# Layer 2's tokens are stored unsummed, and each pass forms Strassen's sums on the chip

## The chip, the core and the metric

The kernel runs on one NeuronCore of one Trainium2 chip. The time is the device time of one execution in microseconds (us). Engines are named as in the profile: PE is TensorE (matmuls; PEld its weight loads), DVE is VectorE, ACT is ScalarE, POOL is GpSimd, SP is the engine whose queue issues every DMA.

## What is computed

Attention in chunks of 64 feeds two gated MLPs, all in float32:

```python
scores = scale * np.matmul(q_c, k_c.transpose(0, 1, 2, 4, 3))   # 8 heads, chunks of 64
attn = softmax(scores)
x = np.matmul(attn, v_c)              # reshaped to 4608 tokens x 512
g = x @ w_gate                        # layer 1: 512 -> 1536 -> 512
x = (g * sigmoid(g)) * (x @ w_val) @ w_out
h = x @ w_in                          # layer 2: 512 -> 2048 -> 512
out = (h * sigmoid(1.702 * h)) @ w_out2
```

## The kernel before

The 4608 tokens are worked on in 9 blocks of 512 (numbers 0 to 8). There are four passes over the blocks: passes 0 and 1 are the two halves of layer 1's hidden width, passes 2 and 3 those of layer 2's. In the trace pass 0 runs to about 460 us (with the attention inside it), pass 1 to about 960 us, pass 2 to about 1290 us, pass 3 to the end. A pass has three groups of weights per block in layer 1 and two in layer 2.

Matrix products are done by Strassen's scheme (Winograd's form): a product of 2x2 quarters takes seven products of quarters or of sums of quarters, labelled "1" to "7". Each float32 operand is split into a high and a low part (`hi` is a rounded copy in float32r, `lo` is the rest), and `mm3` (L628 to L630) makes three matmuls of each pair of operands: hi x hi, hi x lo, lo x hi. So a block's tokens appear as seven tiles `xs` (ring `x`, seven places, one set), each with a hi and a lo half.

What happens to layer 2's tokens before the change: at the end of each block of pass 1 the block lies in `xr`, and `x_to_dram` makes the seven operands. `token_combos` does four subtractions (DVE, L620 and L1048), then each of the seven gets a copy (hi, on ACT, L616, into the staging area `sp`) and a subtraction (lo, in place), and both halves are stored to `x_dram[1]`: 14 stores of 256 KB. Block 7 is an exception: its seven tiles stay in `xs` as pass 2 starts with it. In passes 2 and 3 `x_load` fetches seven tiles of 512 KB for each other block. The area `sp` is also where layer 1's hidden values get their hi and lo halves for the second product (`hidden_part`).

Second weights: a layer 2 pass has two groups, each with seven tiles of second weights of 512 KB (`od_b`). Those of the first group are held for the pass in `WO` (places `wa2`, `wb2`, `wc6` to `wc8`); those of the second group are fetched for every block through the three buffers of ring `o`. In pass 1 the second weights come the same way (`o<-yw_dram`).

While pass 1 runs, layer 2's weights are also converted from the host's form and stored (`group_to_dram`: raw loads, ACT and DVE work, hi and lo into ring `ws` of two buffers, stores `wd_b` and `od_b`); the weights of pass 3 are converted during pass 2.

The order of the instructions is set by a planner (`Program`): every operation is recorded with an engine, a cost, a due time and its dependences, the planner orders each engine's queue, and the table `PLACES` then moves single operations by number ("behind:what" for each engine, and so also from one engine to another). Each engine runs its queue strictly in that order.

Of the kernel before, what the change touches and what calls it, by code (L numbers as in the profile page):

```python
# [9 lines left out]
F32 = mybir.dt.float32  # L10
F32R = mybir.dt.float32r
# [8 lines left out]
P = 128  # L20
# [3 lines left out]
def rd(ap):  # L24
# [1731 lines left out]
```

## Time and profile before

| what | value |
|---|---|
| time, median of 3 runs | 1671.15 us (1670.75 to 1671.49) |
| profiled execution | 1678.61 us, its span 1676.8 us, mean granted clock 0.997 |
| busy share of PE, DVE, ACT, POOL | 98%, 77%, 54%, 31% |
| moved by DMA | 511.85 MB, mean 305 GB/s |

The profiled execution is 7.46 us longer than the median of the runs; differences of the two kernels are taken on the profiled one and carried over. "Busy" of PE is from a model of pipelined matmuls; a stretch in which PE runs without a hole shows its busy time equal to its length, and the number of instructions in it then gives PE's full pace.

### The profile page before, as it was taken

The numbers are of one execution on the slowest core, as the hardware profiler recorded it, in microseconds if no ns is written. First come the engines' busy times: TensorE is split into PE (matmuls) and PEld (weight loads), VectorE is DVE, ScalarE is ACT, GpSimd is POOL, SyncE is SP. The second block draws the span as 40 slices with busy tenths as digits, with TensorE's granted clock in tenths as the row PEclk, the third lists the DMA queues.
The fourth block names the chain that finished last, engine by engine and source line by source line (L and its number), as shares of the span: only waits on it lengthen the run. The fifth ranks groups of instructions, "written<-read, shape, count | busy, mean of one in ns | idle before, by whom it ended". The sixth has DMA issues, their size and how long they took to land. (4 is left out here: it accounts for less than half of the span.)

```text
span 1676.8 us, 38536 instructions
## 1 busy us (share of the span) xinstructions
PE 1639.5 (98%) x15254; PEld 1604.5 (96%) x15254; DVE 1292.6 (77%) x2061; ACT 902.6 (54%) x1574; POOL 517.7 (31%) x505
## 2 busy tenths in 40 slices
PE   8999999999999999999999999999999999999998
PEld 7898999999999999999999999999999999999998
DVE  7998888888887788888887878787865565555556
ACT  6976776767644444445443455566534444444443
POOL 2432433142012311342220232545642133333333
PEclk9999999999999999999999999999999999999999
DMA  7589989998999999999999998898869877777783
GB/s 296 170 284 352 317 270 316 327 309 281 344 378 370 343 356 364 363 371 357 364 343 371 386 343 315 286 329 302 298 244 365 304 226 228 238 232 241 238 277 113
DMA packets 203331, 511.85 MB, mean 305 GB/s; under 512 B 21008, under 2 KB 58896, under 8 KB 202896
## 3 DMA queue, kind: packets, MB, share of 16 engines
q1 hardware_dynamic: 203152, 509.40, 87.0%
q8 instruction: 120, 1.97, 0.4%
q14 instruction: 59, 0.48, 0.1%
HBM read 363.04 MB, written 146.28 MB: 304 GB/s over the span
## 5 line engine op out<-in xcount | busy, mean ns | idle before, releaser
L628 PE MATMUL banks<-xs,wc 128*128 128x256 f32 x1044 | 298.5, 286 | 3.9 <-ACT u L616 3.2
L620 DVE TENSOR_TENSOR c<-u,banks 128x512 f32<-128x512 f32 x312 | 211.8, 683 | 112.2 <-PE banks L630 101.5
L630 PE MATMUL banks<-xs,wc 128*128 128x256 f32 x1044 | 295.2, 283 | 0.0
L629 PE MATMUL banks<-xs,wc 128*128 128x256 f32 x1044 | 295.1, 283 | 0.0
L628 PE MATMUL banks<-xs,wb 128*128 128x256 f32 x744 | 212.1, 285 | 6.9 <-ACT u L616 5.4
L628 PE MATMUL banks<-sp,o 128*128 128x256 f32 (+1 forms) x702 | 210.6, 300 | 5.2 <-DMA o<-yw_dram 4.4
L628 PE MATMUL banks<-xs,wa 128*128 128x256 f32 x744 | 211.6, 284 | 1.1 <-DVE c L620 1.1
L629 PE MATMUL banks<-sp,o 128*128 128x256 f32 (+1 forms) x702 | 207.4, 295 | 4.1 <-DVE sp L620 4.0
L630 PE MATMUL banks<-xs,wa 128*128 128x256 f32 x744 | 210.0, 282 | 0.0
L630 PE MATMUL banks<-xs,wb 128*128 128x256 f32 x744 | 209.8, 282 | 0.0
L629 PE MATMUL banks<-xs,wb 128*128 128x256 f32 x744 | 209.7, 282 | 0.0
L629 PE MATMUL banks<-xs,wa 128*128 128x256 f32 x744 | 209.4, 282 | 0.0
L616 ACT COPY u<-banks 128x512 f32<-128x512 f32 x226 | 131.7, 584 | 142.9 <-PE banks L630 141.8
L628 PEld LDWEIGHTS banks<-xs,wc 128*128 128x128 f32 x1044 | 198.8, 190 | 8.7 <-ACT u L616 6.7
L630 PE MATMUL banks<-sp,o 128*128 128x256 f32 (+1 forms) x702 | 206.0, 293 | 0.0
L629 PEld LDWEIGHTS banks<-xs,wc 128*128 128x128 f32 x1044 | 199.5, 191 | 0.3
L630 PEld LDWEIGHTS banks<-xs,wc 128*128 128x128 f32 x1044 | 199.5, 191 | 0.0
L1258 ACT ACTIVATE xr<-c 128x512 f32<-128x512 f32 x140 | 87.9, 631 | 154.8 <-DVE c L620 134.7
L628 PEld LDWEIGHTS banks<-xs,wb 128*128 128x128 f32 x744 | 141.2, 190 | 9.8 <-ACT u L616 6.7
L628 PEld LDWEIGHTS banks<-xs,wa 128*128 128x128 f32 x744 | 141.4, 190 | 3.0 <-DVE c L620 1.9
L628 PEld LDWEIGHTS banks<-sp,o 128*128 128x128 f32 x702 | 133.0, 189 | 10.6 <-DMA o<-yw_dram 6.0
L629 PEld LDWEIGHTS banks<-xs,wa 128*128 128x128 f32 x744 | 141.3, 190 | 0.5
(289 smaller groups left out, 4728.8 us busy)
## 6 DMA issues: line engine op xcount, KB each, us to landing
xs<-x_dram SPq DMA_DIRECT2D x168, 512.0 KB, 5.7
o<-yw_dram SPq DMA_DIRECT2D x150, 512.0 KB, 5.9
o<-od_b SPq DMA_DIRECT2D x119, 512.0 KB, 4.6
x_dram<-xs SPq DMA_DIRECT2D x63, 512.0 KB, 5.8
wd_b<-ws SPq DMA_DIRECT2D x56, 256.0 KB, 5.0
od_b<-ws SPq DMA_DIRECT2D x56, 256.0 KB, 5.2
raw<-in_moe_w_out SPq DMA_DIRECT2D x56, 255.8 KB, 5.3
x_dram<-sp SPq DMA_DIRECT2D x49, 256.0 KB, 5.5
```

Source lines behind the costliest of these rows:

```text
L616: o = op(eng, us, lambda: on[o.eng](dst.ap, cut(src.ap)), [src], [dst], prio, near=near)
L620: lambda: {"dve": nc.vector, "pool": nc.gpsimd}[o.eng].tensor_tensor(out=dst.ap, in0=of_a(a.ap), in1=of_b(b.ap), op=by), reads or [a, b], ...
L628: nc.tensor.matmul(o, ah, bh, start=first, stop=False, **kind)
L629: nc.tensor.matmul(o, ah, bl, start=False, stop=False, **kind)
L630: nc.tensor.matmul(o, al, bh, start=False, stop=last, **kind)
L1258: op("act", act_us(512), lambda: nc.scalar.activation(out=h.ap, in_=c.ap, func=AF.Gelu_apprx_sigmoid), [c], [h], prio, "gelu")
```

## The change

`x_to_dram` now stores a block of pass 1 as it is, in two stores of 512 KB to the new `x2_dram` (block 7 is as before). In passes 2 and 3 the new `x2_made` takes the place of `x_load` for all blocks but block 7: it loads the two halves of the block (512 KB each) into `wc7` and `wc8`, forms the sums there in place with four subtractions, and makes the seven hi and lo tiles in `xs`. It runs 8 times in pass 2 and 7 times in pass 3. `wc7` and `wc8` held two of the seven resident second weights; those two (index 3 and 4) are now fetched for each block through ring `o`. The table `PLACES` is another one throughout, from pass 0 on.

```diff
-        "4:15,44,24,18 61:7,21,27 78:9,23,19,28 16:52 17:12,11,25,10,14,6,5,69 20:13,26 54:71 7038:244,209,210,86 "
+        "61:14,78,25,28 11:22 12:10,9 15:20,18 24:21,5,27,69,6,17,7,19 26:13 54:71 7027:244,209,210,86 7028:103 "
...
-    def seven_places(j):
+    def seven_places(j, left_out=()):
         a, b = [ring[w + str(j)].new([P, 2, 2, 2, 256], F32R) for w in ("wa", "wb")]
-        c = [ring["wc%d" % (3 * j + i)].new([P, 2, 2, 256], F32R) for i in range(3)]
+        c = [None if 2 + i in left_out else ring["wc%d" % (3 * j + i)].new([P, 2, 2, 256], F32R) for i in range(3)]
...
-            WO[gs[0]] = seven_load(2, gs[0], OD, [prio + (1 + i / 7) * step - 15 for i in range(7)])
+            WO[gs[0]] = seven_load(2, gs[0], OD, [prio + (1 + i / 7) * step - 15 for i in range(7)], (3, 4))
...
     def x_to_dram(xb, b, prio):
-        made = []
-        combos = token_combos(xb, prio)
...
-            copy(hi, src, 512, prio + n, "act", cut)
-            made.append(hi)
-        for n, (m, src, cut) in enumerate(combos):
-            i, hi, eng = ORDER[2].index(m), made[n], ("pool", "dve")[(n + b // (NB - 1)) % 2]
...
-            for c, s in enumerate((hi, lo)):
-                store(x_dram[1][:, b, i, c * 512:(c + 1) * 512].rearrange("p (a t) -> p a t", a=2), s, [xd[1][b][i].part(None)], prio + n + 2)
+        if b < NB - 2 or b == NB - 1:
+            for j in range(2):
+                store(x2_dram[:, b, j], Buf(lambda j=j: xb.ap[:, 2 * j:2 * j + 2].rearrange("p a t -> p (a t)"), None, None, xb),
+                      [x2d[b][j]], prio + 1)
             return
...
+    def x2_made(p, b, prio):
+        made = {m: ring["x"].new([P, 2, 2, HT], F32R) for m in ORDER[2]}
+        X[p, b] = [made[m] for m in ORDER[2]]
+        raw = [ring["wc%d" % (7 + j)].new([P, 2, BT]) for j in range(2)]
+        for j in range(2):
+            load(raw[j].part(lambda ap: ap.rearrange("p a t -> p (a t)")), x2_dram[:, b, j], prio - 10 + j, [x2d[b][j]])
+
+        def side(n):
+            return lambda ap: ap[:, :, n * HT:(n + 1) * HT]
+
+        def parts(m, src, cut=lambda ap: ap):
+            split(*[made[m].part(lambda ap, c=c: ap[:, c]) for c in range(2)], src, 512, prio + ORDER[2].index(m), ("pool", "dve")[m in "257"], cut)
+
+        r0, r1 = raw
+        for m, r, n in (("1", r0, 0), ("2", r1, 0), ("3", r1, 1)):
+            parts(m, r, side(n))
+        t1, t3, t4 = [Buf(lambda r=r, n=n: side(n)(r.ap), None, None, r) for r, n in ((r0, 0), (r0, 1), (r1, 0))]
+        t2 = ring["x1"].new([P, 2, HT])
+        tt(t1, r0, r0, ALU.subtract, 512, prio, of_a=side(1), of_b=side(0), reads=[r0, made["1"]])
+        tt(t2, r1, t1, ALU.subtract, 512, prio, of_a=side(1))
+        parts("6", t2)
+        tt(t3, r1, r0, ALU.subtract, 512, prio + 1, of_a=side(1), of_b=side(1), reads=[r0, r1, t1])
+        parts("7", t3)
+        parts("5", t1)
+        tt(t4, t2, r1, ALU.subtract, 512, prio + 3, of_b=side(0), reads=[t2, r1, made["2"]])
+        parts("4", t4)
...
-                                if g in WO:
+                                if g in WO and WO[g][n] is not None:
...
-                    x_load(nxt[0], BLOCKS[nxt[0]][nxt[1]], start[nxt[0]][nxt[1]] - 18)
+                    if nxt[0] > 1 and BLOCKS[nxt[0]][nxt[1]] != NB - 2:
+                        x2_made(nxt[0], BLOCKS[nxt[0]][nxt[1]], start[nxt[0]][nxt[1]] - 14)
+                    else:
+                        x_load(nxt[0], BLOCKS[nxt[0]][nxt[1]], start[nxt[0]][nxt[1]] - 18)
```

Since the new lines push the file down, a line of the changed kernel has a higher number: L616 and L620 are L666 and L670 there, L608 and L611 are L658 and L661, L1428 is L1494.

How the orders stand against each other is shown at three places. The first is ACT's queue inside pass 1, between the 23rd and the 24th silu of the upper hidden half (`sx<-c`); `sp<-xr` and `sp<-sr` are the token copies of `x_to_dram`, `u<-banks` empties a PSUM bank of layer 1's first product. Before:

```order
637 L1428 ACTIVATE sx<-c 128x2x256
638 L616 COPY u<-banks 128x512
639 L616 CAST ws<-t 128x256
640 L1428 ACTIVATE sh<-c 128x2x256
641 L616 COPY u<-banks 128x512
642 L616 CAST sp<-xr 128x512 x2
643 L616 CAST sp<-sr 128x512
644 L616 COPY u<-banks 128x512
645 L1428 ACTIVATE sx<-c 128x2x256
```

The same place in ACT's queue of the changed kernel, from its 23rd to its 24th `sx<-c`:

```order
637 L1494 ACTIVATE sx<-c 128x2x256
638 L755 ACTIVATE raw<-raw,offset 128x256
639 L666 COPY u<-banks 128x512 x2
640 L666 CAST ws<-st 128x256
641 L1494 ACTIVATE sh<-c 128x2x256
642 L666 CAST ws<-t 128x256
643 L753 ACTIVATE t<-raw,offset 128x256
644 L1494 ACTIVATE sh<-c 128x2x256
645 L666 COPY u<-banks 128x512
646 L666 CAST sp<-sh 128x768
647 L755 ACTIVATE raw<-raw,offset 128x256
648 L1494 ACTIVATE sx<-c 128x2x256
```

The three token copies are gone from between the copies `u`; the copies into `ws` (converted weights) stay.

The second place is DVE's queue where pass 1 goes over into pass 2, around the first rows `c<-u,banks` of the first block of pass 2. `xr<-xr,banks` are the last additions to block 8, `sr<-xr`, L1048 and `sr<-xr,sr` the sums of `token_combos` on it. Before:

```order
1286 L620 TENSOR_TENSOR xr<-xr,banks 128x2x256 x3
1287 L620 TENSOR_TENSOR sp<-sf,sp 128x512
1288 L620 TENSOR_TENSOR sr<-xr 128x512
1289 L1048 TENSOR_TENSOR xr<-xr 128x2x256
1290 L620 TENSOR_TENSOR c<-u,banks 128x512
1291 L620 TENSOR_TENSOR sr<-xr,sr 128x512
1292 L620 TENSOR_TENSOR sf<-t,sf 128x512
1293 L620 TENSOR_TENSOR t<-t 128x512
1294 L620 TENSOR_TENSOR sp<-t,sp 128x512
1295 L620 TENSOR_TENSOR c<-u,banks 128x512
```

DVE at the same place in the changed kernel:

```order
1284 L670 TENSOR_TENSOR c<-u,banks 128x512
1285 L670 TENSOR_TENSOR ws<-st,ws 128x256
1286 L670 TENSOR_TENSOR xr<-xr,banks 128x2x256 x2
1287 L670 TENSOR_TENSOR sp<-sf,sp 128x512
1288 L670 TENSOR_TENSOR sp<-t,sp 128x512
1289 L670 TENSOR_TENSOR sf<-t,sf 128x512
1290 L670 TENSOR_TENSOR t<-t 128x512
1291 L670 TENSOR_TENSOR c<-u,banks 128x512
```

The three sums are gone, and a `c<-u,banks` now stands ahead of the last additions to `xr`.

The third place is DVE's queue around three rows `c<-u,banks` late in pass 3 (in the second last block). Before:

```order
1848 L620 TENSOR_TENSOR sr<-xr,sr 128x512
1849 L620 TENSOR_TENSOR t<-t,banks 128x512
1850 L620 TENSOR_TENSOR sx<-xr,sx 128x512
1851 L620 TENSOR_TENSOR c<-u,banks 128x512
1852 L620 TENSOR_TENSOR sp<-xr,sp 128x512
1853 L620 TENSOR_TENSOR c<-u,banks 128x512
1854 L620 TENSOR_TENSOR sp<-xr,sp 128x512
1855 L620 TENSOR_TENSOR c<-u,banks 128x512
```

DVE at the same place in the changed kernel (`wc_20186` and `wc_20190` are the two halves of the loaded tokens):

```order
2055 L670 TENSOR_TENSOR sf<-wc_20190,wc_20186 128x512
2056 L670 TENSOR_TENSOR c<-u,banks 128x512
2057 L670 TENSOR_TENSOR u<-u,c 128x512
2058 L670 TENSOR_TENSOR t<-t,banks 128x512
2059 L670 TENSOR_TENSOR xs<-sf,xs 128x512
2060 L670 TENSOR_TENSOR c<-u,banks 128x512
2061 L670 TENSOR_TENSOR xs<-wc_20186,xs 128x512
2062 L670 TENSOR_TENSOR sp<-xr,sp 128x512
2063 L670 TENSOR_TENSOR xs<-wc_20190,xs 128x512
2064 L670 TENSOR_TENSOR c<-u,banks 128x512
```

The subtractions of `x2_made` and one that POOL did before (`u<-u,c`) stand between the rows that empty PSUM.

Counted over both whole orders, DVE has 2270 instructions for 2063, ACT 1616 for 1576, POOL 387 for 510, and SP issues 1176 rows for 1315. PE's 14064 matmuls are the same. Of the 15 runs of `x2_made`, DVE got 136 of the 165 subtractions (POOL 29), and ACT 88 of the 105 copies (POOL 17).

## Rows read from the trace of the kernel before

**Rows 1.** The page's first lines: span, and each engine's busy us, share and instructions.

```profile
span 1676.8 us, 38536 instructions
PE 1639.5 (98%) x15254; PEld 1604.5 (96%) x15254; DVE 1292.6 (77%) x2061; ACT 902.6 (54%) x1574; POOL 517.7 (31%) x505
```

**Rows 2.** Busy time by stretch: length, PE, PEld, DVE, ACT, POOL, clock, DMA share, GB/s.

```profile
50.00:250.00 200.00, 198.50 (x2375) 181.83 (x2374) 175.74 (x311) 151.53 (x256) 72.43 (x80) 1.00 0.82 280
460.00:700.00 240.00, 237.50 (x1970) 235.32 (x1969) 201.29 (x324) 110.21 (x200) 45.43 (x49) 1.00 1.00 362
700.00:900.00 200.00, 193.29 (x1577) 190.34 (x1576) 168.13 (x263) 86.86 (x159) 54.07 (x53) 0.99 1.00 361
900.00:1000.00 100.00, 95.59 (x772) 92.64 (x771) 77.63 (x117) 44.56 (x77) 21.26 (x18) 1.00 1.01 371
1000.00:1100.00 100.00, 98.83 (x822) 97.96 (x821) 81.89 (x133) 56.39 (x109) 42.42 (x51) 1.00 0.88 301
1100.00:1300.00 200.00, 200.00 (x1679) 199.81 (x1678) 146.23 (x217) 102.63 (x190) 90.50 (x95) 1.00 0.87 308
1300.00:1600.00 300.00, 300.00 (x2521) 299.95 (x2520) 173.65 (x247) 138.79 (x233) 96.36 (x71) 1.00 0.76 243
```

**Rows 3.** PE's waits, 465 to 1000 us: us in total, times, longest.

```profile
PE banks L628 <- ACT u L616: 4.3, 6, 1.9
PE banks L628 <- DMA o<-yw_dram: 3.2, 6, 1.3
```

**Rows 4.** Busy time by stretch around PE's longest wait of pass 1.

```profile
850.00:853.00 3.00, 1.00 (x7) 0.83 (x7) 0.85 (x3) 0.99 (x3) 0.00 (x0) 1.00 1.03 407
853.00:855.00 2.00, 2.00 (x11) 2.00 (x12) 1.93 (x3) 1.20 (x3) 0.00 (x0) 0.60 1.04 387
```

**Rows 5.** Timeline of ACT: start, us, then in brackets the idle time before and its releaser.

```profile
594.61 0.62 ACT L616 CAST sp<-sr 128x512 fp32r<-128x512 f32 x1 [2.71 <-DMA x_dram<-sp]
852.01 0.40 ACT L616 CAST ws<-st 128x256 fp32r<-128x256 f32 x1 [6.19 <-DMA od_b<-ws]
921.62 0.59 ACT L616 COPY u<-banks 128x512 f32<-128x512 f32 x1 [0.34 <-PE banks L630]
```

**Rows 6.** ACT's waits, 465 to 960 us.

```profile
ACT sp L616 <- DMA x_dram<-sp: 22.0, 15, 3.3
ACT ws L616 <- DMA od_b<-ws: 17.4, 7, 6.2
```

**Rows 7.** PE's waits, 1000 to 1600 us.

```profile
PE banks L628 <- DMA o<-od_b: 0.4, 1, 0.4
```

**Rows 8.** Timeline at the turn to pass 2: two of DVE, two of PE.

```profile
961.40 1.09 DVE L620 TENSOR_TENSOR sr<-xr 128x512 f32<-128x512 f32 x1
...
963.13 0.68 DVE L620 TENSOR_TENSOR c<-u,banks 128x512 f32<-128x512 f32 x1
...
963.87 0.39 PE L628 MATMUL banks<-xs,wb 128*128 128x256 f32 x1 [0.89 <-DVE c L620]
967.00 0.38 PE L628 MATMUL banks<-xs,wa 128*128 128x256 f32 x1 [0.73 <-DVE c L620]
```

**Rows 9.** Groups by line and form: busy us, mean ns, idle before; 50 to 460 us, then 1300 to 1600 us.

```profile
L616 ACT CAST xs<-xr 128x512 fp32r<-128x512 f32 x42 | 25.4, 618 | 6.7 <-PE banks L630 4.3 <-DMA x_dram<-xs 1.3 <-DVE xr L620 0.8
L620 DVE TENSOR_TENSOR xs<-xr,xs 128x512 fp32r<-128x512 f32 x26 | 19.5, 754 | 2.0 <-ACT xs L616 2.0
L620 DVE TENSOR_TENSOR sp<-xr,sp 128x512 fp32r<-128x512 f32 x30 | 20.8, 692 | 29.7 <-ACT sp L616 29.7
```

**Rows 10.** PE's waits, 50 to 460 us.

```profile
PE banks L913 <- ACT xs L616: 0.2, 1, 0.2
```

**Rows 11.** Timeline of POOL and of DVE beside it.

```profile
842.41 1.91 POOL L620 TENSOR_TENSOR sh<-sh,sx 128x768 f32<-128x768 f32 x1
...
842.54 0.68 DVE L620 TENSOR_TENSOR c<-u,banks 128x512 f32<-128x512 f32 x1
843.13 2.00 DVE L620 TENSOR_TENSOR sp<-sh,sp 128x768 fp32r<-128x768 f32 x1
```

More of the change, by code (lines that the diff above doesn't have):

```diff
@@ L29 @@
     "pe": (
[36 rows of a table removed]
[40 rows of a table added]
     ),
     "dve": (
[66 rows of a table removed]
[92 rows of a table added]
     ),
     "act": (
[42 rows of a table removed]
[56 rows of a table added]
     ),
     "pool": (
[13 rows of a table removed]
+        "2:0,120 114:131,132 126:158,164 159:170 177:226,238 349:392 351:407,403 355:395 348:458 512:558,559 "
+        "526:527 531:704 701:705 710:707,762 798:801 804:984,988 811:996,938,939,943 904:1219 "
+        "911:1228,1235,1222,1243 1072:1265,1277 1079:1080 1077:1295,1086 1087:1089,1151 1460:1148 1482:1465 "
+        "1153:1157 1160:1564 1164:1593,1359 1377:1747,1762,1759,1770,1774 1378:1796 1508:1825,1826,1515,1513,1520 "
+        "2039:2045,2057,2054 2050:2062,2084,2095 1887:2258 3320:3651 3656:3873,3871,3979,3982 "
+        "4104:4113,4105,4018,4019,4041,4068 4289:4140 4290:4159,4166,4169,4172 4307:4217,4260 4305:4252,4331 "
+        "4328:4341 4396:4349,4356,4358 4401:4445,4411 4582:4531 4583:4521,4539,4550,4675,4689 4585:4665 4593:4756 "
+        "4603:4717 4601:4788,4790,4864,4869 4711:4725,4832 4715:4956 4729:4975 4904:4907 4908:5101 5133:5092,5146 "
+        "4917:5136,5166,5169,5163,5247 5305:5019,5380,5381 5371:5487 5203:5481 5030:5482,5205 5201:5209 5513:5526 "
+        "5216:5544,5543 5330:5599,5678 5348:5689 5349:5691,5742,5760,5761 5797:5803 5842:5804,5811,5812,5826 "
+        "5861:5829,5848 5866:5868,5921,5922,5891,5899 5924:5900,5944,5956,5957,5995 5945:5965 6061:6068 "
+        "6069:6071,6073,6044 6098:6118,6219,6221,6222,6216 6167:6196,6197,6203 "
+        "6301:6270,6271,6372,6374,6368,6342,6379,6354,6356,6359 6454:6401,6530,6526,6478,6531,6480 "
+        "6528:6522,6505,6511,6512 6536:6556,6607 6557:6577,6590 6631:6674,6659,6660,6662 6689:6665,6760,6722 "
+        "6710:6835,6838 6779:6786,6833,6801,6808,6837,6817 6860:6819,6862,6875 6863:6882,6890,6895,6899,6896 "
+        "6940:6972"
     ),
     "dma": (
[43 rows of a table removed]
[46 rows of a table added]
     ),
@@ L866, in out_pair, with seven_load @@
         return fn
-    def seven_load(j, g, src, prios):
-        made = seven_places(j)
+    def seven_load(j, g, src, prios, left_out=()):
+        made = seven_places(j, left_out)
         d, done = zip(*src[g])
         for i, (b, prio) in enumerate(zip(made, prios)):
-            load(b.part(lambda ap: ap.rearrange("p a b c -> p (a b c)")), d[i][:, i].rearrange("p a b c -> p (a b c)"),
+            if b is not None:
+                load(b.part(lambda ap: ap.rearrange("p a b c -> p (a b c)")), d[i][:, i].rearrange("p a b c -> p (a b c)"),
                  prio, [done[i]])
@@ L1107, in x_load @@
             load(x.part(lambda ap: ap.rearrange("p c a t -> p (c a t)")), x_dram[layer - 1][:, b, i], prio + 2 * i, [xd[layer - 1][b][i]])
+    x2_dram = pool["dram"].tile([P, NB, 2, 2 * BT], F32, name="x2_dram")
+    x2d = [[Buf(None) for j in range(2)] for b in range(NB)]
     def x_to_dram(xb, b, prio):
-        made = []
-        combos = token_combos(xb, prio)
-        if b == NB - 2:
-            X[2, b] = [None] * 7
-            for n, (m, src, cut) in enumerate(combos):
-                i = ORDER[2].index(m)
-                X[2, b][i] = x = ring["x"].new([P, 2, 2, HT], F32R)
-                split(*[x.part(lambda ap, c=c: ap[:, c]) for c in range(2)], src, 512, prio + n, ("dve", "pool")[n % 2], cut)
-                store(x_dram[1][:, b, i], Buf(lambda x=x: x.ap.rearrange("p c a t -> p (c a t)"), None, None, x), [xd[1][b][i]], prio + n + 2)
-            return
@@ L1120, in x_to_dram @@
-        of = {m: src for m, src, cut in combos}
-        for n, (m, src, cut) in enumerate(combos):
-            if b < NB - 1:
-                t = stage["sp"].take(n % 4 * 3, 2)
-                hi = Buf(lambda t=t: t.ap.rearrange("p (a t) -> p a t", a=2), t.prev, t.before, t)
-            else:
-                hi = ring[("ws", "raw")[n % 2]].new([P, 2, HT], F32R)
-            copy(hi, src, 512, prio + n, "act", cut)
-            made.append(hi)
-        for n, (m, src, cut) in enumerate(combos):
-            i, hi, eng = ORDER[2].index(m), made[n], ("pool", "dve")[(n + b // (NB - 1)) % 2]
-            lo = Buf(lambda src=src, cut=cut: cut(src.ap).bitcast(F32R), None, None, src)
-            tt(lo, src, hi, ALU.subtract, 512, prio + n, eng, of_a=cut, of_b=rd,
-               reads=[hi, *(of[k] for k in {"1": "5", "2": "4", "6": "4", "5": "67", "3": "67"}.get(m, ""))])
-            for c, s in enumerate((hi, lo)):
-                store(x_dram[1][:, b, i, c * 512:(c + 1) * 512].rearrange("p (a t) -> p a t", a=2), s, [xd[1][b][i].part(None)], prio + n + 2)
+        if b < NB - 2 or b == NB - 1:
+            for j in range(2):
+                store(x2_dram[:, b, j], Buf(lambda j=j: xb.ap[:, 2 * j:2 * j + 2].rearrange("p a t -> p (a t)"), None, None, xb),
+                      [x2d[b][j]], prio + 1)
+            return
@@ new lines, in x_to_dram @@
+        X[2, b] = [None] * 7
+        for n, (m, src, cut) in enumerate(token_combos(xb, prio)):
+            i = ORDER[2].index(m)
+            X[2, b][i] = x = ring["x"].new([P, 2, 2, HT], F32R)
+            split(*[x.part(lambda ap, c=c: ap[:, c]) for c in range(2)], src, 512, prio + n, ("dve", "pool")[n % 2], cut)
+            store(x_dram[1][:, b, i], Buf(lambda x=x: x.ap.rearrange("p c a t -> p (c a t)"), None, None, x), [xd[1][b][i]], prio + n + 2)
+    def x2_made(p, b, prio):
[21 more added lines that the diff above has]
+        parts("4", t4)
```

432 rows, old and new, of the table PLACES are left out of this document.

## The prediction

> **What bounds the kernel now.** The page's first lines come first: PE is busy for 98% of the span, DVE for 77%, ACT for 54% [rows 1]. PE's matmuls are the same before and after, so a gain can only come from the time in which PE stands still or runs slowly. The busy times by stretch say where that is [rows 2]. From 1300 to 1600 us PE is busy the whole time and makes 2521 matmuls in 300 us, so its full pace is 0.1190 us for one. I take the other stretches against it: length less count times 0.1190. From 460 to 700 us 5.6 us are lost (240 less 1970 x 0.1190), from 700 to 900 us 12.3, from 900 to 1000 us 8.1, from 1000 to 1100 us 2.2, from 1100 to 1300 us 0.2. So nearly all that can be won lies in pass 1 and the turn to pass 2: 26.0 us. Passes 2 and 3, into which the change puts work, lose next to nothing now. The idle time in the three stretches from 460 to 1000 us sums to 2.50 + 6.71 + 4.41 = 13.6 us, so a microsecond of waiting costs 1.9 in all: PE starts again slowly after each wait, and once the granted clock fell. After PE's longest wait it stood at 0.60 on average from 853 to 855 us, so mostly at the lower of its two levels (1.2 GHz instead of 2.4), with 11 matmuls in 2 us instead of 17 [rows 4]. I use 1.9 as the price of waiting.
>
> What the waits are for stands in PE's waits [rows 3]: 4.3 us for ACT's copies `u` and 3.2 us for second weights `o`, which DMA brings late. ACT is not short of time there (110 us busy of 240 [rows 2]). Its own timeline shows why it is late: its queue stands still behind a copy whose target buffer is not yet stored, 2.71 us for `x_dram<-sp` before the `u` at 595 us and 6.19 us for `od_b<-ws` before the `u` for which PE waits longest [rows 5]. DMA's share is 1.00 in those stretches and 0.88 from 1000 us on [rows 2]. So pass 1 is bounded by PE with holes, and the holes come mainly from a full DMA queue. One of the six late `u`, at 922 us, had waited for PE itself [rows 5]; I put the other five sixths, 3.6 of the 4.3 us, down to DMA.
>
> **The change part by part.**
>
> *Pass 1, stores.* Eight blocks lose 14 stores of 256 KB and get two of 512 KB, 2.5 MiB less each, 21 MB in all. The rates of the three stretches give 0.24 ms x 362 + 0.20 x 361 + 0.10 x 371 = 196 MB, so DMA's share falls by 11%, to about 0.9. That is where 1000 to 1100 us stands today (0.88), and there and later PE waits once for a DMA, 0.4 us [rows 7]; at 1.9 that is 0.8 us per 100, or 4.1 us over the 540 us. Today it is (3.2 + 3.6) x 1.9 = 12.9 us. Term: -8.8 us. Bounds: 0, if the stores of converted weights alone keep the queue full, and -12.9.
>
> *Pass 1, engines.* Seven copies and eleven subtractions a block go. Of ACT's own waits, those on `x_dram<-sp` (22.0 us) go with them, those on `od_b<-ws` (17.4) stay [rows 6]; this is inside the term above. The new table gives what DVE is spared to work that POOL had, so I count nothing for DVE in pass 1; the cover is that DVE is busy 84% there, as today [rows 2].
>
> *The turn to pass 2.* PE waited 0.89 and 0.73 us for rows `c<-u,banks` which stood in DVE's queue behind sums of block 8's tokens, the first of 1.09 us [rows 8]. The order has them gone, and the first `c` ahead of the other work too. The first wait should go, of the second a half: -(0.89 + 0.36) x 1.9 = -2.4 us. Bounds 0 and -3.1.
>
> *Passes 2 and 3, engines.* A run of `x2_made` gives DVE 136/15 = 9.1 subtractions, ACT 5.9 copies, POOL 2.7 operations. By the nearest rows a subtraction takes 0.69 us (late in the kernel) and a copy 0.62 [rows 9]: 6.3 us of DVE and 3.6 us of ACT for a block, which PE needs 336 x 0.1190 = 40 us for. In pass 3 DVE goes from 58% to about 74%, below the 82% at which 1000 to 1100 us runs today; nothing is lost. In pass 2, from 1000 to 1300 us, DVE is busy 82 + 146 = 228 us of 300 [rows 2]; 7.5 blocks add 47 us, and a share of the 146 instructions that POOL hands over elsewhere (300/1677 of them at 0.69) another 18: 293 us of 300, less what DVE no longer waits for POOL. No row shows PE beside so full a DVE. The nearest is 50 to 250 us: DVE 88%, ACT 76%, PE idle 1.5 us [rows 2], so 4.3 us over 300 at 1.9, against the 2.4 us of today. Term: +1.9. Bounds: -2.4 (no hole left), and +22, if pass 2 loses what 900 to 1000 us loses today (8.1 us per 100).
>
> Are the tiles `xs` themselves late? The same building in place runs in pass 0 for every block (`x_made`; the copies and subtractions of [rows 9]), with DVE as full, and no matmul of a product is named as waiting on it; the one wait on `xs` is of attention, 0.2 us [rows 10]. Taken as nothing, inside the bounds above.
>
> *Second weights.* Nine loads through `o` for a block instead of seven, but four loads of 512 KB in place of seven for tokens and these two: DMA's share falls below 0.87 and 0.76. PE waited 0.4 us for seven loads a block [rows 7]; two more cost 0.2 at most at 1.9. If they waited as often as those of pass 1 (3.2 us in some 165 loads), 34 more would cost 1.3. Taken: 0.
>
> *The table in pass 0.* Its order changes without new work. Either sign is open; taken 0, bounds plus and minus 3 us, twice what PE stands idle from 50 to 250 us [rows 2].
>
> Sum: -8.8 - 2.4 + 1.9 = -9.3 us, so the profiled execution goes from 1678.6 to 1669.3 us, and the median from 1671.15 (it lies 7.5 us below the profiled one) to **1662** us.
>
> **A row and a rule on the port.** From 842.41 us POOL runs for 1.91 us. DVE's `c<-u,banks`, which reads PSUM, takes its usual 0.68 us beside it; the next, which reads two tiles of SBUF, starts at 843.13 and takes 2.00 us, the 1.19 us until POOL is done and 0.81 more [rows 11]. Between 1100 and 1300 us POOL is busy 45% and DVE 73%, and PE loses 0.2 us, so this lock is already paid for in DVE's busy time there and hides. The Trainium skill (SBUF — State Buffer, "SBUF: two separate sides") says that DVE and GpSimd share a pair of ports as an exclusive lock for a whole instruction, and that a DVE operation with two SBUF inputs waits for it. By that rule each of the 9.1 subtractions would stand behind POOL with the chance 0.45 for half of the mean 0.95 us (90.50 us in 95 operations), 15 us more for 7.5 blocks: DVE would need 308 us of 300, and the sum would be that of the second rival below.
>
> **The rivals.**
>
> *More is won.* All that DMA delays goes, the turn gets clean, and DVE's halves `sp` come earlier as the area is no longer shared with the token copies; pass 2 stays without holes. -12.9 - 3.1 - 2.4 = -18 us: 1653. For it: POOL's disturbance of DVE leaves pass 1. Against: the stores `wd_b` and `od_b` stay, and the longest wait was theirs [rows 5].
>
> *DVE becomes the bound in pass 2: slower.* It is the 293 us of 300 above. If what POOL no longer disturbs gives less than some 8 us back, rows `c<-u,banks` queue behind sums and conversions, as at 963 us [rows 8], and PE loses at the rate of 900 to 1000 us: +22 us there, -11 from pass 1, so 1682. It decides where DVE's busy share in 1000 to 1300 us passes 95%. Against it: 1100 to 1300 us has 73% and no loss at all, and POOL's own share falls.
>
> *No change.* The queue stays full with weight conversions and ACT keeps standing behind `ws`: a third of the DMA term (-4), -2 at the turn, and pass 2 loses 6 us more: 1671.
>
> **How the numbers follow.** The forecast case (1658 to 1667) has 0.46, more won 0.20, no change 0.18, slower 0.16. Cutting off the ends of the first and last rival leaves 1653 to 1674 with 8 in 10. About 0.2% (3.3 us) is what a measurement of this kernel tells from no change: faster 0.66, within 0.18, slower 0.16.
>
> **What would show it.** Right: DMA's share from 460 to 960 us at or below 0.93; PE's waits for `u` and `o` there below 3 us together; ACT without waits on `x_dram`; more matmuls than 1577 from 700 to 900 us; 1100 to 1300 us still with some 1675. Wrong: PE's waits on `c` or on `sp` between 1000 and 1300 us with DVE above 95%; waits on `xs` with ACT or DVE as the releaser at the start of a block; waits on `o<-od_b`; or pass 0 losing more than 3 us by the new order.

## The result: 21.5 us faster, more than twice the forecast

The changed kernel takes 1649.77 us (median of 4 runs, 1648.6 to 1652.28), the kernel before 1671.32 us beside it (1670.75 to 1671.77): ratio 0.9873, 95% interval 0.9856 to 0.989. The forecast was 1662 us, with a range down to 1653.

The page's first lines of the changed kernel, to be read against [rows 1]:

```profile
span 1650.5 us, 38198 instructions
PE 1629.6 (99%) x15254; PEld 1602.9 (97%) x15254; DVE 1367.1 (83%) x2268; ACT 906.4 (55%) x1614; POOL 400.5 (24%) x382
```

PE makes the same 15254 matmuls. Its busy time by stretch, with the columns of [rows 2]:

```profile
460.00:700.00 240.00, 238.82 (x1993) 237.66 (x1993) 191.21 (x329) 106.08 (x197) 2.72 (x3) 1.00 0.95 339
700.00:900.00 200.00, 199.17 (x1671) 198.99 (x1670) 159.07 (x269) 76.58 (x140) 3.73 (x5) 1.00 0.95 330
900.00:1000.00 100.00, 98.81 (x824) 98.11 (x823) 88.10 (x139) 57.99 (x106) 27.98 (x25) 1.00 0.87 300
1000.00:1100.00 100.00, 100.00 (x841) 100.00 (x840) 88.41 (x145) 61.79 (x118) 32.41 (x32) 1.00 0.73 239
1100.00:1300.00 200.00, 199.80 (x1672) 199.25 (x1671) 168.52 (x289) 120.94 (x234) 53.50 (x51) 1.00 0.82 280
1300.00:1600.00 300.00, 299.78 (x2510) 299.15 (x2509) 231.89 (x343) 135.83 (x234) 111.89 (x98) 1.00 0.65 211
```

I use the measure of the prediction, length less matmuls times 0.1190 us, over pass 1 and the turn together (460 to 1100 us). Before, 640 less 5141 x 0.1190 is 28.2 us [rows 2]; after, 640 less 5329 x 0.1190 is 5.8 us. So 22.4 us come from there. From 1100 to 1600 us the loss goes from 0.2 us [rows 2] to 2.3 us. The profiled execution of before was 7.5 us above its median, so differences of traces come out somewhat larger here than those of medians.

PE's waits from 465 to 1000 us, to be read against [rows 3], are nearly gone; no `u` is among them (L678 is the first matmul of `mm3` here):

```profile
PE banks L678 <- DMA xs<-x_dram: 1.1, 2, 0.8
PE banks L678 <- DVE c L670: 0.9, 1, 0.9
PE banks L678 <- DMA o<-yw_dram: 0.9, 4, 0.3
```

What does not fit the forecast is DMA's share: 0.95, not 0.9, and yet hardly a hole is left. ACT's own wait for stores of weights, `ws`, is not gone either, from 465 to 960 us:

```profile
ACT ws L666 <- DMA wd_b<-ws: 22.8, 10, 3.9
```

Behind the last matmul a little is won too. Before, two additions on POOL stand ahead of the last output stores; after, one of the two is on DVE. Timeline of POOL before, then of POOL and DVE after:

```profile
1670.85 2.48 POOL L620 TENSOR_TENSOR t<-t,sf 128x512 f32<-128x512 f32 x2
```

```profile
1644.48 1.29 POOL L670 TENSOR_TENSOR t<-t,sf 128x512 f32<-128x512 f32 x1
...
1645.86 0.69 DVE L670 TENSOR_TENSOR t<-t,sf 128x512 f32<-128x512 f32 x1
```

### The profile page after: what moved, and what is told of

It is laid out like the page before. It is cut to its first block, busy times and chain, and to the rows that moved or that the text cites. A ratio compares the mean times of both kernels' runs of the same rounds, so it can differ in the third digit from the quotient of the medians.

```text
span 1650.5 us, 38198 instructions
## 1 busy us (share of the span) xinstructions
PE 1629.6 (99%) x15254; PEld 1602.9 (97%) x15254; DVE 1367.1 (83%) x2268; ACT 906.4 (55%) x1614; POOL 400.5 (24%) x382
## 4 chain that ended last, share of the span: by engine, by line
PE 90%; DMA 7%; DVE 1%; ACT 1%; SPq 0%; issue 0%; DVEq 0%; ACTq 0%
PE banks L678 30%; PE banks L680 29%; PE banks L679 29%; DMA o<-yw_dram 2%; PE banks L964 1%; DMA xs<-x_dram 1%; PE banks L959 1%; DMA sp<-in_k 1%; PE banks L1029 1%; DMA wd_a<-ws 1%; DMA wd_b<-ws 1%; DMA o<-od_b 0%; DMA sr<-in_k 0%; DMA sr<-in_v 0%; DVE c L670 0%
## 5 line engine op out<-in xcount | busy, mean ns | idle before, releaser
L678 PE MATMUL banks<-xs,wc 128*128 128x256 f32 x1044 | 298.1, 286 | 6.2 <-DVE c L670 3.3
L670 DVE TENSOR_TENSOR c<-u,banks 128x512 f32<-128x512 f32 x312 | 211.9, 684 | 80.1 <-PE banks L680 66.9
L678 PE MATMUL banks<-xs,wb 128*128 128x256 f32 x744 | 211.8, 285 | 1.3 <-ACT u L666 0.9
L678 PE MATMUL banks<-xs,wa 128*128 128x256 f32 x744 | 211.5, 284 | 0.0
L678 PE MATMUL banks<-sp,o 128*128 128x256 f32 (+1 forms) x702 | 209.3, 298 | 1.8 <-DMA o<-yw_dram 1.8
L666 ACT COPY u<-banks 128x512 f32<-128x512 f32 x203 | 118.6, 585 | 166.1 <-PE banks L680 149.7
L678 PEld LDWEIGHTS banks<-xs,wc 128*128 128x128 f32 x1044 | 199.8, 191 | 9.5 <-ACT u L666 3.1
L678 PEld LDWEIGHTS banks<-xs,wb 128*128 128x128 f32 x744 | 141.3, 190 | 3.8 <-ACT u L666 1.8
L679 PEld LDWEIGHTS banks<-xs,wb 128*128 128x128 f32 x744 | 141.3, 190 | 1.2 <-DVE xs L670 0.8
L678 PEld LDWEIGHTS banks<-xs,wa 128*128 128x128 f32 x744 | 141.1, 190 | 1.4 <-issue 0.2
```

Source lines behind the costliest of these rows:

```text
L666: o = op(eng, us, lambda: on[o.eng](dst.ap, cut(src.ap)), [src], [dst], prio, near=near)
L670: lambda: {"dve": nc.vector, "pool": nc.gpsimd}[o.eng].tensor_tensor(out=dst.ap, in0=of_a(a.ap), in1=of_b(b.ap), op=by), reads or [a, b], ...
L678: nc.tensor.matmul(o, ah, bh, start=first, stop=False, **kind)
L679: nc.tensor.matmul(o, ah, bl, start=False, stop=False, **kind)
```

## The experiments

Three theories: **A**, the bytes of the token stores fill the DMA queue; **B**, the copies and subtractions of the tokens hold up ACT and DVE; **C**, the new order of the instructions (the table) removes holes that the work itself would have left. The prediction was A, with 0 for B and for C. "Lost" is the measure above, 460 to 1100 us, in each run's own trace; in kernels far slower than before it is rough, since other work stands in those microseconds. A single trace gives it to some 4 us: up to 900 us e6_turn has the work and the order of before, and from 460 to 900 us it loses 14.2 us where before loses 17.9 (440 us less 3578 and 3547 x 0.1190). Each run is compared with the kernel before that ran beside it.

| run | median us (runs) | before beside it | ratio, 95% interval | lost us |
|---|---|---|---|---|
| before | 1671.32 (4) | | | 28.2 |
| changed kernel | 1649.77 (4) | 1671.32 | 0.9873 (0.9856 to 0.989) | 5.8 |
| e1_sliver | 1665.66 (9) | 1674.12 | 0.9953 (0.9937 to 0.997) | 18.0 |
| e2_traffic | 1709.02 (4) | 1674.12 | 1.0215 (1.0185 to 1.0245) | 63.2 |
| e3_before_no_table | 1723.64 (4) | 1674.12 | 1.0299 (1.026 to 1.0338) | 33.7 |
| e3_after_no_table | 1721.26 (4) | 1674.12 | 1.0279 (1.0247 to 1.0311) | 16.3 |
| e4_spread | 1685.48 (4) | 1673.15 | 1.0074 (1.0048 to 1.01) | 43.7 |
| e5_light | 1664.07 (5) | 1673.15 | 0.9947 (0.9928 to 0.9966) | 16.2 |
| e6_turn | 1670.95 (10) | 1673.15 | 0.9977 (0.9963 to 0.9992) | 23.5 |
| e7_old_order | 1670.05 (10) | 1672.28 | 0.9984 (0.9971 to 0.9996) | 23.3 |
| e8_joined | 1663.59 (6) | 1673.48 | 0.9929 (0.9904 to 0.9954) | 14.8 |
| e9_old_engines | 1741.77 (4) | 1672.28 | 1.0421 (1.0396 to 1.0447) | 19.3 |
| e10_new_order | 1757.13 (4) | 1672.28 | 1.0509 (1.0489 to 1.053) | 110.9 |
| e11_new_order_light | 1707.01 (4) | 1672.28 | 1.0208 (1.0191 to 1.0225) | 57.9 |
| e12_old_to_900 | 1660.42 (4) | 1673.48 | 0.9912 (0.9879 to 0.9946) | 13.7 |
| e13_old_pass0 | 1652.55 (4) | 1673.48 | 0.9867 (0.9831 to 0.9902) | 4.7 |
| e14_new_sp | 1716.53 (4) | 1676.19 | 1.0254 (1.0216 to 1.0292) | 74.0 |
| e15_old_sp | 1722.58 (4) | 1676.19 | 1.0294 (1.0261 to 1.0326) | 77.7 |
| e16_old_pool | 1656.29 (4) | 1676.19 | 0.989 (0.9866 to 0.9915) | 11.7 |

### The stores alone

In the kernel before, each token store writes a quarter of its bytes. (In this run and in e5_light and e11_new_order_light layer 2 works on the tokens that layer 1 stored; in e6_turn it does so for the last block.)

```
-                store(x_dram[1][:, b, i, c * 512:(c + 1) * 512]..., s, ...)
+                op("dma", ..., lambda: nc.sync.dma_start(out=dst[:, :1, :128], in_=bits(s.ap[:, :1, :128])), ...)
```

> The kernel before, with each of the 14 token stores of a block in pass 1 cut to its first 64 KB of 256 KB; layer 2 then reads layer 1's stored tokens instead, so its output is of other tokens. All engine work, the table and the number of DMAs stay. Theory A (the bytes of the token stores fill the DMA queue of pass 1, and that makes the holes of PE): 12 to 18 us faster than before, PE's progress through pass 1 gains at least 10 us. Theory B (the copies and sums of the tokens on ACT and DVE make the holes): 0 to 3 us faster. Theory C (the new table, which takes POOL's work out of pass 1 and orders all queues anew, made the gain): 0 to 3 us faster.

8.5 us by the medians, 5 to 10.5 by the interval; my 12 to 18 for theory A missed. It is the size of the forecast's term for the stores (-8.8), and not half of the whole gain. By stretch, DMA's share falls to where the forecast put it:

```profile
460.00:700.00 240.00, 237.36 (x1979) 236.10 (x1978) 202.47 (x327) 111.08 (x201) 47.01 (x52) 1.00 0.93 330
700.00:900.00 200.00, 198.12 (x1647) 196.63 (x1646) 170.51 (x266) 90.50 (x164) 51.61 (x51) 1.00 0.92 321
```

The waits do not follow the forecast's working. All of PE's waits from 465 to 1000 us in e1_sliver, and then those on `c` and `sp` in the kernel before, which stand there beside [rows 3]:

```profile
PE banks L628 <- DMA o<-yw_dram: 3.2, 4, 1.6
PE banks L628 <- DVE c L620: 2.7, 3, 1.1
PE banks L628 <- ACT u L616: 2.3, 3, 1.1
PE banks L630 <- DVE sp L620: 0.9, 1, 0.9
```

```profile
PE banks L628 <- DVE c L620: 1.9, 3, 0.9
PE banks L629 <- DVE sp L620: 1.8, 4, 0.6
PE banks L630 <- DVE sp L620: 1.1, 2, 0.9
```

The waits for `u` fall from 4.3 to 2.3 us and those for `sp` from 2.9 to 0.9; those for `o` stay at 3.2, and those for `c` rise from 1.9 to 2.7.

### The engines' work on top, and the last block alone

The kernel before again: stores cut to slivers, and the eleven subtractions and seven copies of a block too (e5_light); then the same for the last block only (e6_turn). The order stays.

```
+        bit = (lambda ap: ap) if b == NB - 2 else lambda ap: ap[:, :1, :8]
-            copy(hi, src, 512, prio + n, "act", cut)
+            copy(hi, src, 512, prio + n, "act", cut, bit=bit)
...
-            tt(lo, src, hi, ALU.subtract, 512, prio + n, eng, of_a=cut, of_b=rd,
+            tt(lo, src, hi, ALU.subtract, 512, prio + n, eng, of_a=cut, of_b=rd, bit=bit,
```

> The kernel before, with the token stores of eight blocks cut to slivers, as before, and the eleven subtractions and seven copies for those tokens cut to 16 numbers a partition as well (layer 2 reads the stored tokens of layer 1); order, number of instructions and layer 2's loads stay. If engine work is what the run with the stores alone still lacked, it goes to 1650 to 1654 us, with pass 1 and the turn both without holes. If the new order of the instructions is needed for it, it stays at 1662 to 1665, as with the stores alone. My prediction (engine work in pass 1 worth 0, turn 2.4) says 1663.

> The kernel before, with the copies, subtractions and stores cut for the last block alone, whose tokens stand at the turn to pass 2. My prediction gave the turn 2.4 us: 1668 to 1669 by the 1671 us of before. If the block's work at the turn is what the changed kernel won there, 7 us go: 1663 to 1665. If the new order won it, no change: 1671.

Taking the work off the engines adds nothing that can be measured to what the stores give (0.9947 against 0.9953; the two intervals leave room for some 4 us). As the main cause B falls. The last block is worth 2.2 us by the medians, 1.3 to 6.2 by the interval, its stores included. In e6_turn's trace both waits for `c` of [rows 8] are gone; e1_sliver, with that block's stores cut and its sums in place, still has both (0.89 and 0.73 us). So the forecast's -2.4 holds, and the 8 us that the changed kernel's trace wins from 900 to 1100 us (1594 matmuls before [rows 2], 1665 after) do not come from that block's work. From 465 to 1000 us PE still waits in e5_light, for DMA above all:

```profile
PE banks L628 <- DMA o<-yw_dram: 3.5, 6, 1.4
PE banks L628 <- ACT u L616: 1.6, 3, 0.7
```

### The traffic put back into the changed kernel

Ten transfers of 256 KB within DRAM for each of eight blocks (21 MB, what the stores lost): in two rows of five behind a block's own stores (e2_traffic), or one or two behind each load of tokens (e4_spread). The edit of e2_traffic:

```
+                    for i in range(5):
+                        nc.sync.dma_start(out=junk_dram[:, b, j, i], in_=x0_dram[:, i % 4 * 512:(i % 4 + 1) * 512])
```

> The changed kernel, with ten more DMAs of 256 KB (DRAM to DRAM, to a place nobody reads) behind the two token stores of each block in pass 1, so that DMA moves at least as many bytes there as before; no engine has more work and nothing waits for them. Theory A: 10 to 16 us slower than the changed kernel, 1660 to 1666 us. Theories B and C: within 3 us of it, 1647 to 1653 us.

> The changed kernel, and behind each of the seven loads of a block's tokens in pass 1 one or two extra transfers of 256 KB within DRAM, ten for a block: the same ten as in the run with the traffic in one place, which lost 59 us, but spread out. If bytes alone decide, the loss is the same 59 us. If it is the place in the queue (ten transfers in a row ahead of the next tokens, for which PE then waited 20.5 us), spread transfers should cost about what the cut stores gave back, 8 to 10 us: 1658 to 1660 us, with waits on o and u of 8 to 10 us and on xs below 3.

By the ratios to before they lose some 57 and 34 us against the changed kernel; both expectations missed. Spreading saves about 23 us, so the place in the queue counts. PE's longest sums of waits, of e2_traffic and then of e4_spread, show it: tokens behind the added rows, or second weights:

```profile
PE banks L678 <- DMA xs<-x_dram: 20.5, 7, 5.3
```

```profile
PE banks L678 <- DMA o<-yw_dram: 17.7, 17, 2.8
```

What the same bytes cost as stores in the order of before was 8 us. Part of the difference may be the kind: in e2_traffic a transfer within DRAM took 7.1 us in the median from issue to landing, a store from SBUF of the same size 5.3:

```profile
junk_dram<-x_dram SPq DMA_DIRECT2D x80, 256.0 KB, 7.1
...
od_b<-ws SPq DMA_DIRECT2D x56, 256.0 KB, 5.3
```

### Without tables

Both kernels in the planner's own order, with the table of places emptied:

```
-PLACES = {
-    "pe": (
...
+PLACES = {}
```

> The kernel before with an empty table, so that the planner's own order stands. All theories: slower than before, by 20 to 60 us. It is the base for the next run: theories A and B say that the changed kernel without its table is 12 to 20 us faster than this one, theory C that it is within 5 us of it or slower.

> The changed kernel with an empty table. Theories A and B: 12 to 20 us faster than the kernel before without its table. Theory C: within 5 us of that or slower, since the gain came with the new table.

The totals differ by 2.4 us, with ranges that overlap, and seem to say that the change is worth nothing without its table. The stretches say more: from 460 to 1100 us the change wins 17.4 us here too (33.7 to 16.3), and from 1100 to 1600 us it loses 11.2 (500 us less 4169 and 4075 x 0.1190: 3.9 and 15.1). Behind 1600 us it loses another 5.2 (121.2 us less 959 and 120.2 less 907 x 0.1190: 7.1 and 12.3), which brings the two spans within 1 us of each other. The forecast's slower rival stands in e3_after_no_table from 1100 to 1300 us:

```profile
1100.00:1300.00 200.00, 196.21 (x1613) 193.09 (x1612) 189.57 (x230) 125.49 (x223) 135.54 (x127) 1.00 0.69 228
```

DVE is busy 95% and PE loses 8.1 us of 200. One DVE instruction takes 0.82 us in the mean beside POOL at 135.54 us; in the changed kernel it takes 0.58 us (168.52 / 289) beside POOL at 53.50. The mix of instructions is not the same, so here are three forms by themselves, from 1100 to 1300 us (busy us, mean ns), in the changed kernel and then in e3_after_no_table (L409 is L670 there):

```profile
L670 DVE TENSOR_TENSOR xs<-wc,xs 128x512 fp32r<-128x512 f32 x20 | 14.2, 711 | 0.0
L670 DVE TENSOR_TENSOR sx<-xr,sr 128x512 fp32r<-128x512 f32 x9 | 6.4, 706 | 0.2 <-ACT sr L666 0.2
L670 DVE TENSOR_TENSOR c<-u,banks 128x512 f32<-128x512 f32 x30 | 20.6, 687 | 15.5 <-PE banks L680 14.6
```

```profile
L409 DVE TENSOR_TENSOR xs<-wc,xs 128x512 fp32r<-128x512 f32 x15 | 14.4, 987 | 0.0
L409 DVE TENSOR_TENSOR sx<-xr,sr 128x512 fp32r<-128x512 f32 x10 | 11.0, 1103 | 0.1
L409 DVE TENSOR_TENSOR c<-u,banks 128x512 f32<-128x512 f32 x29 | 19.6, 677 | 0.9 <-PE banks L419 0.8
```

The two that read two tiles of SBUF take 0.28 and 0.40 us longer beside the busier POOL; `c<-u,banks`, which reads PSUM, does not.

### The change in the order of before

The changed kernel, with its instructions up to a certain point in the order, and on the engines, that they have in the kernel before (the removed ones left out): up to the first products of pass 2 (e7_old_order; e8_joined), to some 50 us before the turn (e12_old_to_900), or for pass 0 only (e13_old_pass0). A list for each engine takes the place of the table:

```
-        queue = {eng: [o for o in seq if o.eng == eng] for eng in self.FREE}
...
+        queue = {eng: [self.ops[n] for n in runs(QUEUES[eng])] for eng in self.FREE}
```

> The changed kernel, with the order and the engines of the kernel before for everything up to the first products of pass 2 (the token copies, subtractions and stores that no longer exist are simply missing there; a block's two new stores stand where its first token store stood). Layer 2 keeps the new order. If the new order of passes 0 and 1 and of the turn won what the missing work did not, some 12 us, it goes to 1661 to 1664 us, with PE's waits on u and o in pass 1 as in the run without token work. If the gain lay in layer 2 or in the work itself: 1649 to 1653.

> The changed kernel in the order of before up to the turn, as in the run before, with the load for the first block of pass 2 that is built in place moved ahead in SP's queue (to where the new order has it beside PE's work). If the stall of 6.9 us was of the join, it and its slow restart go: 1657 to 1662. If the old order as such costs the 20 us, 1667 to 1671.

> The same, with the old order only to some 50 us before the turn (near 920 us); the turn in the new order. If the new order's worth is at the turn (DVE's rows c there), most of the gain is back: 1650 to 1654. If it is in pass 1, no more than 3 us below the run with the old order through the turn: 1655 to 1660.

> The same, with the old order for pass 0 alone. The prediction took the new order of pass 0 as 0 plus or minus 3; by the traces it is worth 2 to 4 us (2.4 of them in the first 50 us): 1651 to 1654. If the whole worth of the order is in pass 0, 1658 or more.

e7_old_order is spoilt by my own join. The load of the first block that is built in place stood behind the whole old queue, and ACT stood still for it from 936 us on, ahead of a `u`:

```profile
ACT xs L748 <- DMA wc<-x_dram: 9.7, 1, 9.7
```

e8_joined mends that and stands 9.9 us below before by the medians (7.7 to 16.1 by the interval): the whole change, without a new order ahead of layer 2, is worth about what was forecast for it (-9.3). Then it goes down by stairs; the three runs have the same runs of before beside them. The turn in the new order gives 3.2 us more, with ranges that overlap. Pass 1 in the new order gives 7.9 us more (1657.49 to 1663.3 in the one, 1651.77 to 1653.05 in the other). The new order of pass 0 gives nothing more (0.9867 against the changed kernel's 0.9873), where I had expected 2 to 4 us. Busy time by stretch and PE's waits from 465 to 1000 us, first of e8_joined (L760 is the matmul of L678):

```profile
460.00:700.00 240.00, 236.39 (x1971) 235.24 (x1970) 181.33 (x296) 99.79 (x180) 35.10 (x44) 1.00 0.92 332
700.00:900.00 200.00, 198.83 (x1655) 197.46 (x1654) 144.02 (x230) 76.22 (x137) 40.12 (x42) 1.00 0.90 324
```

```profile
PE banks L760 <- DMA o<-yw_dram: 4.6, 7, 1.5
PE banks L760 <- ACT u L748: 3.7, 5, 1.9
```

and of e13_old_pass0 (L761 is that matmul):

```profile
460.00:700.00 240.00, 238.42 (x1994) 237.71 (x1993) 194.08 (x330) 101.72 (x187) 8.85 (x10) 1.00 0.95 338
700.00:900.00 200.00, 200.00 (x1678) 199.81 (x1677) 159.53 (x270) 77.06 (x141) 4.06 (x6) 1.00 0.94 334
```

```profile
PE banks L761 <- DVE c L753: 1.4, 3, 0.9
PE banks L761 <- DMA o<-yw_dram: 1.4, 2, 1.1
```

The same transfers keep DMA busier and let PE wait less. What the order of the turn is worth shows by stretch too, here of e8_joined and then of e12_old_to_900:

```profile
900.00:1000.00 100.00, 95.50 (x787) 93.93 (x787) 86.70 (x140) 52.50 (x96) 21.64 (x20) 1.00 0.89 320
1000.00:1100.00 100.00, 100.00 (x841) 100.00 (x841) 86.23 (x144) 61.27 (x117) 30.27 (x30) 1.00 0.72 234
```

```profile
900.00:1000.00 100.00, 98.80 (x823) 98.04 (x822) 88.30 (x138) 56.11 (x103) 27.88 (x25) 1.00 0.86 300
```

From 900 to 1000 us the new order makes 36 matmuls more, 4.3 us at 0.1190. From 1000 to 1100 us 841 are made with either order of the turn, where before makes 822 [rows 2]: that part comes with the changed kernel's layer 2.

### The new order in the kernel before

The other way round: the kernel before, complete, in the changed kernel's order up to the turn, its token work beside the same products as in its own (e10_new_order); and with the token work cut as in e5_light (e11_new_order_light).

> The kernel before, complete, but in the changed kernel's order and engines up to the first products of pass 2; its token copies, subtractions and stores stand beside the same products as before. If the new order is a gain of its own, 12 us come here too: 1659 to 1662. If it pays only where the token work is gone (DVE has POOL's work and the tokens' together), nothing is won or it is slower: 1671 to 1685.

> The same with the token copies, subtractions and stores cut to slivers: the changed kernel's passes 0 and 1, with the old layer 2. If missing work and new order together are the whole gain, 1648 to 1652; if the changed kernel's layer 2 costs what its trace lost there (2.5 us), 1646 to 1650; if something else is in the gain, 1655 or more.

The order is no gain of its own: it costs 85 us with the token work in place, far more than I had expected, and 35 us with that work cut to slivers. In both the halves `sp`, whose area the token copies share, stand out. ACT's waits for token stores out of that area come to 40.5 us in e10_new_order, where they were 22.0 [rows 6], and to 38.3 us in e11_new_order_light, though there such a store has only 4 KB. PE's waits in e11_new_order_light begin with `sp`. The two rows of ACT, then that of PE:

```profile
ACT sp L748 <- DMA x_dram<-sp: 40.5, 12, 6.4
```

```profile
ACT sp L748 <- DMA x_dram<-sp: 38.3, 10, 6.1
```

```profile
PE banks L760 <- ACT sp L748: 11.8, 4, 4.3
```

I had expected 1648 to 1652 us of the second. The places that I gave the token copies in the new order are mine, and a better choice may cost less; but the copies, however small, keep their places in the area and in ACT's queue. Nor was a table fitted anew for the kernel before, without the change, tried.

### What in the new order does it

Four kernels with parts of the two orders: on their old engines, all instructions of passes 0 and 1 in the new order (e9_old_engines); SP's queue alone exchanged (e14_new_sp, e15_old_sp); POOL's work alone given back from pass 1 to the turn (e16_old_pool). The edit is again to the lists.

> The changed kernel in its own order, but in passes 0 and 1 each instruction on the engine that it had before: POOL takes 136 instructions back from DVE and ACT and gives 62 away. If the new order works by keeping POOL out of pass 1, the time goes up by 6 us or more, to 1656 to 1664. If the sequence alone does it, 1649 to 1653.

> The changed kernel with PE, DVE, ACT and POOL in the order and on the engines of before up to the turn, SP's queue alone in the new order from pass 1 on. If the order of the transfers is what pays, PE's waits on o<-yw_dram in pass 1 go from 4.6 us (all in the old order, 1663.6) to below 2, and the time to 1653 to 1657. If the engines' order pays, 1661 to 1665.

> The other way round: the changed kernel with SP's queue alone in the old order from pass 1 to the turn. If the order of the transfers pays, 1658 to 1663, with waits on o<-yw_dram of 3 us or more; if the engines' order does, 1650 to 1654.

> The changed kernel in its own order; from pass 1 to the turn only the 77 instructions that the new order took from POOL go back to it, and 8 that it gave to POOL go back to DVE and ACT, each at its place in the order of before. If POOL's slower instructions were what was late, 1656 to 1664, with waits on what POOL makes; if the sequence or SP's queue pays, 1650 to 1654.

e9_old_engines is inconclusive: it loses most of its time in pass 0 already (2173 matmuls from 250 to 460 us, the changed kernel 2362), where nothing was in question. The exchange of SP's queue tells nothing apart either: against the changed kernel it costs over 60 us whichever side is old. PE's longest waits from 465 to 1000 us are then for engines and transfers alike, in e14_new_sp and in e15_old_sp:

```profile
PE banks L760 <- ACT u L748: 15.1, 7, 9.0
PE banks L760 <- DMA o<-yw_dram: 10.5, 13, 2.6
```

```profile
PE banks L762 <- DVE sp L753: 13.5, 4, 7.2
PE banks L761 <- DVE c L753: 13.2, 3, 7.7
```

The expectations of these three runs, 1649 to 1665 us over all their cases, missed. So the order of the transfers and that of the engines are fitted to each other. With POOL's 77 instructions back the time is not told apart from the changed kernel's by the ratio (0.989 against 0.9873, overlapping), though its trace loses 11.7 us instead of 5.8, mostly behind two waits:

```profile
PE banks L761 <- DMA o<-yw_dram: 2.8, 1, 2.8
PE banks L761 <- DVE c L753: 2.7, 2, 2.2
```

## Why the prediction was wrong

**Stores (-8.8): right in size, in part by luck.** e1_sliver gave 8.5 us, with DMA's share at 0.92 to 0.93. The working let PE's waits for `u` and `o` fall by 4.6 us (8.8 / 1.9). In e1_sliver those for `u` fell by 2.0 and those for `o` not at all; another 2.0 came from the halves `sp`, which only the rival "more is won" had named. In e8_joined `u` and `o` stand at 8.3 us together, above the 7.5 of before, while PE's whole idle time from 460 to 1000 us falls from 13.6 to 9.3 us. The prediction's own sign, `u` and `o` below 3 us together, is met only in the new order.

**Engines in pass 1 (0): right, as far as the runs can tell.** e5_light against e1_sliver: no difference, to some 4 us.

**Turn (-2.4): right for the work that leaves it.** e6_turn gave 2.2 us, and both waits for `c` are gone from its trace.

**Passes 2 and 3 (+1.9): inside the bounds, with the wrong sign.** The term was for 1000 to 1300 us. There the loss fell from 2.4 us [rows 2] to 1.0 (300 less 2513 x 0.1190); from 1300 to 1600 us, taken as nothing, it rose from 0.0 to 1.3. Over both it stayed where it was. And DVE is busy 257 us of 300 from 1000 to 1300 us (88.41 + 168.52), not 293. I had priced every instruction at 0.69 us; 72 more in 1100 to 1300 us (289 for 217) brought only 22 us, since the mean fell from 0.67 [rows 2] to 0.58 us while POOL's busy time fell from 90.50 to 53.50. The slower rival is real: in e3_after_no_table, with POOL at 135.54 us, DVE reaches 95% and PE loses 8.1 us. In the changed kernel POOL has less work there, and DVE 84% (168.52 of 200). The Trainium skill (SBUF — State Buffer, "SBUF: two separate sides") lets a DVE operation with two SBUF inputs wait for a whole POOL instruction that holds the port; the three means, 0.58, 0.67 and 0.82 us beside POOL at 53.50, 90.50 and 135.54 us of 200, go the way that it says. So do the single forms: `xs<-wc,xs` takes 0.71 us in the changed kernel and 0.99 in e3_after_no_table.

**`xs`, second weights, the table in pass 0 (0): right.** From 1100 to 1600 us PE waits 0.2 us for a second weight and 0.2 us for a `t`; e13_old_pass0 shows no worth of pass 0's order.

**The step that failed** is the one on the table, whose worth in pass 1 was a term at nothing. The prediction took the new order as 0 in pass 0, and in pass 1 only as work handed from POOL to DVE ("so I count nothing for DVE in pass 1"). Beyond the rows of the turn it worked as if the rest of the order stood still: what DMA still delays was left in as 4.1 us, and the holes not put down to DMA stayed. In the order of before the sum comes out (e8_joined, 9.9 us faster where 9.3 were forecast), though not by the waits that it was summed from. The new order then takes away 7.9 us more in pass 1 and some 3 at the turn, so half of the gain; PE's waits for `u` are gone with it and those for `o` fall to 0.9 us.

That half seems to belong to the removal all the same. The new order does not pay with the token work in place (e10_new_order), nor with its copies merely shortened (e11_new_order_light), in the one placement of that work that was tried; and with the planner's own order in both kernels the change wins 17.4 us from 460 to 1100 us, in one trace each. That no other table would have won something in the kernel before is not shown. Of the rivals "more is won" came nearest, with clean waits and a clean turn, but it too was summed from the waits that I put down to DMA; the rest had no price.

Nor was DMA's share the right sign of lateness: at 0.89 to 0.92 PE waits 4.6 us for second weights (e8_joined), at 0.87 to 0.95 it waits 0.9 us (the changed kernel). The price of a wait held roughly: from 460 to 1000 us the changed kernel's PE is idle 3.2 us and loses 5.9, a factor of 1.8 where I used 1.9; in e8_joined it is idle 9.3 us and loses 14.9, a factor of 1.6.

**Open:** what in the new order of pass 1 is decisive. It was not to be had apart from the rest: with SP's queue in the one order and the engines in the other the loss was larger than the whole gain, whichever way round, and of POOL's part (between nothing and 6 us) the interval is too wide. The small gain behind the last matmul was seen in the traces and not tried by itself.

## What to carry to other kernels

Where an order is fitted to the work, removing work has two prices: what the old order gives back, whose size the waits and rows of the old profile told here, and what a new order can do with the room, which they did not. The first came within 1 us of the forecast by the medians (its interval is 7.7 to 16.1), the second was as large; so give the re-fitted order a term of its own wherever the change touches a full queue, bounded by all idle time of that stretch and its restarts (26.0 us here, of which 20.1 went), not only by the waits put down to what was removed. And compare two kernels by stretch, not by their totals: without tables the change seemed to be worth 2.4 us by the medians, and by the traces it was 17.4 us won up to 1100 us and 16.4 lost behind it.

## What was not expected of the hardware

Taking 21 MB of stores out of a queue at a share of 1.00 gave 8 us; putting 21 MB of transfers within DRAM into one at 0.95 cost 34 us spread out and 57 us in rows. One DVE instruction took 0.58, 0.67 or 0.82 us in the mean, from 1100 to 1300 us, as POOL was busy 27%, 45% or 68% of the time beside it; the mix of instructions differs too, so not all of that is POOL's. Of the single forms those that read two tiles of SBUF grew, from 0.71 to 0.99 and to 1.10 us, and `c<-u,banks`, which reads PSUM, stayed at 0.69 and 0.68 us.
